# Reordering the loads and TensorE's work of batch 1 in a fused linear-attention and SwiGLU kernel

## The chip, the cores and the metric

The kernel runs on one core of a Trainium2 chip. The metric is the device time of one execution in microseconds (us), the median of several executions of the same program.

Engines: PE is TensorE's matmul stream and PEld its weight loads, DVE is VectorE, ACT ScalarE, POOL GpSimd, SP SyncE (which issues nearly all transfers here, 143 of 148 in the kernel before). A name with a q (SPq, PEldq) is an engine's sequencer. "L515" is a line of the kernel; the changed kernel's lines are higher by one or two.

## The reference, cut to what matters

```python
# q, k, v: (8 batches, 8 heads, 576 tokens, 64); weights 512 x 1536, 512 x 1536, 1536 x 512
kv  = einsum('bhsd,bhse->bhde', k, v)          # "states": one 64x64 matrix per head
out = einsum('bhsd,bhde->bhse', q, kv)
x   = out / sqrt(mean(out**2, -1) + 1e-6) * g_norm      # per head; then heads side by side: 4608 x 512
xn  = x / sqrt(mean(x**2, -1) + 1e-6) * moe_rms_g
y   = (silu(xn @ w_gate) * (xn @ w_val)) @ w_out        # 4608 x 512
```

All inputs and the output are fp32. The kernel computes in bf16 with fp32 accumulation.

## The kernel before

The work goes in nine units of 512 tokens (eight batches, then their tails together). A unit has 12 *up* steps (gate and value products, SiLU, product) and 48 *down* products. While PE does one unit's products, the attention of the next batch is slipped in between. The first unit has no unit ahead of it under which to hide the loads and preparations, so its order is written out by hand. The change touches that hand-written part: the first 57 of 324 us.

The parts that matter, shortened ("..." marks cuts):

```python
def load_wo(blk):                        # out weights come in three blocks of 4 chunks (1 MB each)
    st = stage()
    ap = st.rearrange("p (c d) -> p c d", d=d_model)
    nc.sync.dma_start(out=ap, in_=wo_view[:, 4 * blk : 4 * blk + 4, :])
    w_st["o", blk] = ap

# order of the loads
load_kv(1, "k", nc.sync); load_wo(0); load_kv(1, "v", nc.sync)
load_q(1); load_wo(1); load_wo(2); load_batch(2)

for j in range(4, NF):                   # up steps of the first unit
    ffn.up(j)
    ...                                  # casts of batch 1's keys and of out weights block 0 in between
for i in range(NS):
    cast_kv(1, "v", i, DVE if i % 2 else SC)
for i in range(4):
    cast_q(1, slice(2 * i, 2 * i + 2), SC if i == 2 else DVE)

def f_cols(j):                           # "columns": (q @ state) turned, one bank each; ACT squares them
    ps = att_pool.tile([128, MAIN], FP32, name="att_ps")       # a pool of two banks
    F.turned(j, ps)
    SC.activation(out=F.sq[:, j, :], in_=ps, func=ACT.Square)

down_part(0, 0, 4); down_part(1, 0, 4)   # down_part(c, lo, hi): chunks lo..hi of 128 tokens number c
att1.kv_products((0, 1, 2, 3)); att1.kv_copy()                 # states of batch 1
down_part(2, 0, 4)
turns.q_turn(0, SC); turns.q_turn(1, DVE)                      # turn of the queries on PE
down_part(3, 0, 4)
round_wo(1, 0, 2, DVE)                   # casts of out weights block 1 ...
...
f_cols(0); f_cols(1)
down_part(0, 4, 6); down_part(1, 4, 6)
f_cols(2); f_cols(3)
down_part(2, 4, 6); down_part(3, 4, 6)
F.sums()                                 # needs all four squares; then the normalisation of unit 1 begins
```

In the traces PE takes this work in the order written, and a group that is not ready holds what follows. In the kernel before, the turn began at 43.71 us and stood while its queries were cast, and the fourth down part, whose out weights the three parts ahead of it had used from 39.8 us on, began behind it, at 45.28.

## Time and profile before

Before: 325.77 us (median of 4 executions, 325.61 to 325.98); the profiled span is 323.6 us. PE is busy for 313.3 us of it (97%), at the full granted clock. The profile of the kernel before lacks the records of 34 of 1925 matmuls.

The windows view of the kernel before; columns are the stretch, its length, busy time and instruction count of each engine, granted PE clock, busy share of the DMA engines, GB/s:

```profile
core 0: us, PE busy (x) PEld busy (x) DVE busy (x) ACT busy (x) POOL busy (x), PEclk, DMA share, GB/s
0.00:26.00 26.00, 21.80 (x244) 14.35 (x248) 17.67 (x53) 14.21 (x27) 9.42 (x25) 1.00 1.00 324
26.00:39.59 13.59, 13.54 (x62) 6.17 (x63) 8.92 (x16) 7.25 (x13) 5.19 (x9) 1.00 1.05 384
39.59:57.00 17.41, 16.69 (x191) 9.30 (x192) 10.78 (x28) 10.44 (x18) 5.30 (x10) 1.00 1.09 332
57.00:300.00 243.00, 241.63 (x1285) 116.60 (x1310) 139.13 (x269) 139.56 (x250) 1.53 (x2) 1.00 0.55 141
```

After 57 us PE is all but full. Ahead of that the DMA engines are full (share 1.0 and more): weights and inputs stream in at 324 to 384 GB/s, and work that waits for a landing hangs on the order of that stream (the values of batch 1 landed at 40.2 us here, behind out weights block 0).

The chain of waits of the kernel before, 28 to 48 us (start, length, what):

```profile
28.11 15.09 DMA st<-in_q_dram
43.22 1.11 DVE qb L108 x3
...
45.48 0.69 DVE qt L108
46.17 0.97 DVE wo_sb L108
...
47.18 1.02 PE o_ps L515 x4
```

The queries of batch 1 land at 43.2 us. From there the chain goes through their casts, the copy of the turned queries and a cast of out weights before PE has work again at 47.18.

The timeline of the kernel before, a few groups of it (start, length, engine, line, operation; in brackets the idle time just before and what ended it):

```profile
41.41 1.32 PE L264 MATMUL att_ps<-vb,kb 64*64 64x64 bf16 x72
43.22 1.10 DVE L108 CAST qb<-st 128x512 bf16<-128x512 f32 x3 [1.56 <-DMA st<-in_q_dram]
43.71 1.74 PE L820 MATMUL att_ps<-identity,qb 128*128 128x128 bf16 x16
45.28 1.03 PE L515 MATMUL v_ps<-wo_sb,h_sb 128*128 128x512 bf16 x4
...
46.09 1.04 DVE L108 CAST wo_sb<-st 128x1024 bf16<-128x1024 f32 x1
46.23 0.60 PE L402 MATMUL att_ps<-qt,kv_all 128*128 128x512 bf16 x2
47.18 1.02 PE L515 MATMUL o_ps<-wo_sb,h_sb 128*128 128x512 bf16 x4 [0.35 <-DVE wo_sb L108]
...
49.62 0.55 PE L418 MATMUL att_ps<-sel,sqt 128*128 128x4 bf16 x16
...
57.01 1.03 PE L471 MATMUL g_ps<-xnt,wg_sb 128*128 128x512 bf16 x3
```

Read starts, not lengths, for PE: a 512-wide matmul is listed with 0.38 us, but the next one starts 0.216 us after it (groups of four follow each other every 0.86 to 0.87 us), so lengths overlap. The turn (L820, 16 small matmuls) holds PE from 43.71 to 45.28, 1.57 us, although such matmuls follow each other every 0.055 us elsewhere (16 of them from 17.62 to 18.51 us), because its queries are still being cast (DVE until 44.32). Two columns at 46.23 would take 0.43 us, but the next group starts at 47.18, when the out weights are cast. The last line, the first up product of the second unit at 57.01, is the milestone.

### The profile page before, as it was taken

The numbers are of one execution on the slowest core, as the hardware profiler recorded it, in microseconds if no ns is written. First come the engines' busy times: TensorE is split into PE (matmuls) and PEld (weight loads), VectorE is DVE, ScalarE is ACT, GpSimd is POOL, SyncE is SP. The second block draws the span as 40 slices with busy tenths as digits, with TensorE's granted clock in tenths as the row PEclk, the third lists the DMA queues.
The fourth block names the chain that finished last, engine by engine and source line by source line (L and its number), as shares of the span: only waits on it lengthen the run. The fifth ranks groups of instructions, "written<-read, shape, count | busy, mean of one in ns | idle before, by whom it ended". The sixth has DMA issues, their size and how long they took to land.

```text
span 323.6 us, 5091 instructions
## 1 busy us (share of the span) xinstructions
PE 313.3 (97%) x1891; PEld 156.5 (48%) x1925; DVE 180.9 (56%) x371; ACT 177.3 (55%) x316; POOL 21.5 (7%) x44
## 2 busy tenths in 40 slices
PE   7799999999999999999999999999999999999995
PEld 3485445554454445444544454444544444444443
DVE  4795756569527842685268616870588058803310
ACT  3476357756756576557665765666554355223321
POOL 1264324200000000000000000000000000000000
PEclk9999999999999999999999999999999999999999
DMA  7999999995279639952794279956101620150014
GB/s 261 347 350 386 379 373 289 250 280 144 54 195 286 151 65 181 303 137 49 189 313 133 46 153 199 312 138 158 69 2 27 151 83 0 21 172 6 0 34 98
DMA packets 75077, 54.87 MB, mean 170 GB/s; under 512 B 42152, under 2 KB 68012, under 8 KB 75052
## 3 DMA queue, kind: packets, MB, share of 16 engines
q1 hardware_dynamic: 74672, 53.88, 60.0%
q10 hardware_dynamic: 380, 0.66, 0.6%
q8 instruction: 15, 0.25, 0.3%
q14 instruction: 10, 0.08, 0.1%
HBM read 37.75 MB, written 9.44 MB: 146 GB/s over the span
## 4 chain that ended last, share of the span: by engine, by line
PE 81%; DMA 10%; DVE 3%; SPq 3%; issue 1%; POOL 0%; ACT 0%; DVEq 0%
PE o_ps L515 25%; PE g_ps L471 24%; PE v_ps L471 24%; DMA st<-in_q_dram 7%; DMA st<-in_moe_w_val_dram 3%; SPq L193 2%; PE att_ps L271 2%; PE att_ps L342 2%; DVE h_sb L477 1%; PE v_ps L515 1%; PE g_ps L515 1%; PE att_ps L337 0%; PE o_ps L552 0%; DVE ssq L360 0%; DVE qb L108 0%
## 5 line engine op out<-in xcount | busy, mean ns | idle before, releaser
L477 DVE TENSOR_TENSOR h_sb<-silu,v_ps 128x512 bf16<-128x512 bf16 x104 | 71.1, 684 | 110.4 <-PE v_ps L471 61.4
L471 PE MATMUL g_ps<-xnt,wg_sb 128*128 128x512 bf16 x403 | 105.1, 379 | 0.8 <-ACT wg_sb L201 0.2
L471 PE MATMUL v_ps<-xnt,wv_sb 128*128 128x512 bf16 x407 | 105.5, 379 | 0.4
L476 ACT ACTIVATE silu<-g_ps 128x512 bf16<-128x512 f32 x104 | 62.5, 601 | 64.1 <-PE g_ps L471 53.4
L515 PE MATMUL o_ps<-wo_sb,h_sb 128*128 128x512 bf16 x387 | 87.0, 379 | 0.8 <-DVE wo_sb L108 0.3
L471 PEld LDWEIGHTS <-wv_sb 128*128 128x128 bf16 x416 | 40.7, 98 | 49.1 <-DVE wv_sb L203 0.2
L515 PEld LDWEIGHTS <-h_sb 128*128 128x128 bf16 x420 | 40.7, 98 | 48.3 <-issue 0.6
L471 PEld LDWEIGHTS <-wg_sb 128*128 128x128 bf16 x416 | 38.7, 98 | 39.9 <-issue 0.3
L106 ACT COPY o_sb<-o_ps 128x512 f32<-128x512 f32 (+1 forms) x34 | 19.7, 579 | 38.1 <-PE o_ps L515 36.3
L360 DVE TENSOR_REDUCE ssq<-sq 128x16 f32<-128x1024 bf16 x28 | 34.1, 1220 | 1.0
L351 ACT ACTIVATE sq<-att_ps 128x512 bf16<-128x512 f32 x28 | 16.7, 597 | 13.7 <-PE att_ps L342 8.7
L106 ACT CAST vb<-st 128x512 bf16<-128x512 f32 (+2 forms) x34 | 19.5, 626 | 5.1 <-DMA st<-in_v_dram 5.1
L377 DVE TENSOR_TENSOR xna<-outa,s1y 128x512 bf16<-128x512 bf16 x28 | 17.5, 685 | 0.2
L353 ACT CAST outa<-att_ps 128x512 bf16<-128x512 f32 x28 | 16.2, 580 | 0.0
L106 ACT CAST qb<-st 128x1024 bf16<-128x1024 f32 (+1 forms) x15 | 14.2, 987 | 3.2 <-DMA st<-in_q_dram 3.2
L106 ACT CAST kb<-st 128x512 bf16<-128x512 f32 (+1 forms) x25 | 14.0, 619 | 0.0
L359 DVE TENSOR_TENSOR sq<-sq,gsq 128x512 bf16<-128x512 bf16 x28 | 11.7, 418 | 0.0
L342 PEld LDWEIGHTS <-qt 128*128 128x128 bf16 x96 | 7.4, 98 | 5.7
L342 PE MATMUL att_ps<-kv_all,qt 128*128 128x128 bf16 x96 | 9.3, 219 | 0.1
L271 PEld LDWEIGHTS <-kb 128*128 128x128 bf16 x120 | 7.7, 98 | 2.8
L612 PE MATMUL att_ps<-kv_all 128*128 128x512 bf16 (+1 forms) x19 | 6.9, 497 | 1.9 <-DVE sel L601 1.2
L271 PE MATMUL att_ps<-vb,kb 128*128 128x128 bf16 x120 | 8.7, 219 | 0.0
(134 smaller groups left out, 164.6 us busy)
## 6 DMA issues: line engine op xcount, KB each, us to landing
out_dram<-o_sb SPq DMA_DIRECT2D x16, 512.0 KB, 3.1
st<-in_q_dram SPq DMA_DIRECT2D x7, 1024.0 KB, 7.6
st<-in_k_dram SPq DMA_DIRECT2D x6, 1024.0 KB, 9.2
st<-in_v_dram SPq DMA_DIRECT2D x6, 1024.0 KB, 11.1
st<-in_moe_w_out_dram SPq DMA_DIRECT2D x3, 1024.0 KB, 13.5
st<-in_moe_w_gate_dram SPq DMA_DIRECT2D x4, 512.0 KB, 9.4
st<-in_moe_w_val_dram SPq DMA_DIRECT2D x4, 512.0 KB, 9.9
st<-in_k_dram SPq DMA_DIRECT2D x4, 288.0 KB, 5.2
```

What stands on the lines that cost most here:

```text
L106: engine.copy(out=dst, in_=src)
L271: PE.matmul(ps, lhsT=bufs[b]["k"][:, t, hs, :], rhs=bufs[b]["v"][:, t, hs, :], start=(first and t == 0), stop=(last and t == T),)
L342: PE.matmul(cols, lhsT=self.qt[:, j, 128 * c : 128 * c + 128], rhs=kv_all[:, self.n, j, :], start=(j == 0), stop=(j == NS - 1),)
L351: SC.activation(out=self.sq[c][:, 0], in_=ps, func=ACT.Square)
L353: SC.copy(out=self.outa[c], in_=ps)
L359: DVE.tensor_tensor(out=sq[:, 1], in0=sq[:, 0], in1=gsq8, op=OP.mult)
L360: DVE.reduce_sum(out=self.ssq[:, c], in_=sq, axis=AX.X)
L377: DVE.tensor_tensor(out=self.xna[c], in0=self.outa[c], in1=self.alpha[:, c, :].to_broadcast([128, H, D]), op=OP.mult)
L471: PE.matmul(ps, lhsT=wt[:, s, j * 128 : (j + 1) * 128], rhs=x[:, s, :], start=(s == 0), stop=(s == NS - 1),)
L476: SC.activation(out=silu, in_=g_ps, func=ACT.Silu)
L477: DVE.tensor_tensor(out=self.h[:, j, :], in0=silu, in1=v_ps, op=OP.mult)
L515: PE.matmul(self.o_ps[c], lhsT=self.h[:, j, c * 128 : (c + 1) * 128], rhs=wo_sb[:, j, :], start=(j == 0), stop=(j == NF - 1),)
```

## The change

Its intent: let everything that waits for a landing wait behind work that does not. The values of batch 1 are loaded ahead of the out weights, so that the states can run as soon as the up steps end; all 16 first down products stand between the states and the turn; out weights come in half loads, so that the first chunks of a block can be cast earlier; and the four columns get four banks, so that they need not wait for squares. At the very start, the gamma row is turned in another bank, and the rounding of one weight block is spread over three engines.

```diff
--- before.py
+++ after.py
@@ -207,7 +207,8 @@
     def load_wo(blk):
         st = stage()
         ap = st.rearrange("p (c d) -> p c d", d=d_model)
-        nc.sync.dma_start(out=ap, in_=wo_view[:, 4 * blk : 4 * blk + 4, :])
+        for i in (0, 2):
+            nc.sync.dma_start(out=ap[:, i : i + 2, :], in_=wo_view[:, 4 * blk + i : 4 * blk + i + 2, :])
         w_st["o", blk] = ap
 
     def round_wo(blk, i, n, engine):
@@ -695,7 +696,7 @@
     cast_kv(0, "v", 2, SC)
     put_q0(0, qps, 0, DVE)
     put_q0(0, qps, 1, SC)
-    gam_ps = att_pool.tile([128, 512], FP32, name="att_ps")
+    gam_ps = ops_pool.tile([128, 512], FP32, name="o_ps")
     PE.matmul(gam_ps[:, 0:5], lhsT=gam[0:5, :], rhs=ident32[0:5, 0:5], is_transpose=True, start=True, stop=True)
     DVE.tensor_copy(out=gcol, in_=gam_ps[:, NS : NS + 1])
     DVE.tensor_scalar(out=rowscale, in0=gam_ps[:, 0:NS], scalar1=gcol[:, 0:1], scalar2=None, op0=OP.mult)
@@ -760,10 +761,10 @@
     round_w(1, "g", 0, SC)
     round_w(1, "g", 3, SC)
     round_w(1, "g", 1, GP)
+    xs = [Z.scale(c, oZ[c]) for c in range(2)]
+    for s, engine in enumerate((GP, SC, DVE, DVE)):
+        round_w(1, "v", s, engine)
     SC.preload_act_table(ACT.Silu)
-    xs = [Z.scale(c, oZ[c]) for c in range(2)]
-    for s in range(NS):
-        round_w(1, "v", s, GP if s < 2 else DVE)
     clear_tail_rows(0, GP)
 
     def turnsZ():
@@ -778,9 +779,9 @@
             load_w(blk, name, nc.sync)
     alloc_kv(1, "k")
     load_kv(1, "k", nc.sync)
-    load_wo(0)
     alloc_kv(1, "v")
     load_kv(1, "v", nc.sync)
+    load_wo(0)
     load_q(1)
     load_wo(1)
     load_wo(2)
@@ -835,19 +836,22 @@
         if j == 6:
             for s in (0, 1):
                 round_w(4, "v", s, DVE)
-        if j >= 8:
-            cast_kv(1, "k", j - 8, DVE)
-        if j == 7:
-            for i in range(4):
-                round_wo(0, i, 1, GP)
-    for i in range(NS):
-        cast_kv(1, "v", i, DVE if i % 2 else SC)
-    for i in range(4):
-        cast_q(1, slice(2 * i, 2 * i + 2), SC if i == 2 else DVE)
+        if j == 9:
+            for i in range(3):
+                cast_kv(1, "k", i, DVE)
+        if j == 10:
+            cast_kv(1, "k", 3, DVE)
+            for i, engine in enumerate((SC, DVE, GP, DVE)):
+                cast_kv(1, "v", i, engine)
+    for i, engine in enumerate((SC, GP, DVE, SC)):
+        round_wo(0, i, 1, engine)
+    for i, engine in enumerate((DVE, SC, DVE, GP)):
+        cast_q(1, slice(2 * i, 2 * i + 2), engine)
     alloc_xnt(1)
 
     def f_cols(j):
-        ps = att_pool.tile([128, MAIN], FP32, name="att_ps")
+        p, nm = ((att_pool, "att_ps"), (att_pool, "att_ps"), (gps_pool, "g_ps"), (vps_pool, "v_ps"))[j]
+        ps = p.tile([128, MAIN], FP32, name=nm)
         F.turned(j, ps)
         SC.activation(out=F.sq[:, j, :], in_=ps, func=ACT.Square)
 
@@ -867,27 +871,21 @@
         round_wo(blk, 0, 2, DVE)
         round_wo(blk, 2, 2, SC)
 
-    down_part(0, 0, 4)
-    down_part(1, 0, 4)
     att1.kv_products((0, 1, 2, 3))
     att1.kv_copy()
-    down_part(2, 0, 4)
+    for c in range(4):
+        down_part(c, 0, 4)
     turns.q_turn(0, SC)
     turns.q_turn(1, DVE)
-    down_part(3, 0, 4)
-    round_wo(1, 0, 2, DVE)
-    for i in (2, 3):
-        round_wo(1, i, 1, GP)
-    for i in range(4):
-        round_wo(2, i, 1, GP)
+    for blk in (1, 2):
+        for i in range(4):
+            round_wo(blk, i, 1, GP)
     clear_tail_rows(1, GP)
     F = Cols(1, 0, 512, turns.qt, sqt_pool.tile([128, NS, MAIN], BF16, name="sqt"), "F")
-    f_cols(0)
-    f_cols(1)
     for c in range(2):
         down_part(c, 4, 6)
-    f_cols(2)
-    f_cols(3)
+    for j in range(NS):
+        f_cols(j)
     for c in range(2, 4):
         down_part(c, 4, 6)
     F.alloc_sums()
```

## The prediction

> **What bounds it.** The page gives PE busy 313.3 of 323.6 us at full granted clock. In the windows view PE is busy 241.6 of 243.0 us from 57 to 300 us; the change leaves that alone. Room is only ahead of 57 us: 26 to 39.6 us PE is busy 13.54 of 13.59 us; 39.6 to 57.0 us (down products and states, turns, columns of batch 1) 16.7 of 17.4, and the timeline shows more stalls inside its groups. That stretch hangs on the input DMA: its 16 engines are 90% busy in nearly all slices to 57 us, and the chain goes from the queries of batch 1 (issued 28.1, landed 43.2 us) over their casts (to 44.33), the turn (45.46), its copy (DVE, to 46.17) and the cast of out weights (DVE, to 47.13) to PE at 47.18.
>
> **Stalls before**, from the timeline: the turn holds PE 43.71 to 45.28, 1.57 us for 16 small matmuls that take 0.055 us each elsewhere (0.9 us): 0.7 lost, as PE reached it during the query casts. Two columns at 46.23, the next down products at 47.18: 0.5 lost to the out weight cast. With smaller gaps about 1.5 us.
>
> **What the change does.** Bytes, matmuls and casts stay. Transfers land 2.75 to 3 us apart per MB (37.3, 40.2, 43.2, 46.0, 48.7). Estimate after: values 37.5, out weights block 0 in halves 38.9 and 40.2, queries 43.2 unchanged (the DMA has a backlog), next halves 44.6 and 46.0. States run at 39.6 us (their casts end near 40.5: perhaps 0.1 lost), then all 16 down products (0.216 us each) to about 44.6. The query casts, now on three engines, end near 44.0, so the turn is stall-free, 44.6 to 45.5; before, turn and 16 products ended at 46.14. About 0.65 us gained. The products of chunks 4 and 5 then come ahead of the columns; POOL casts these chunks (0.63 us each) 44.6 to 45.9, so PE may lose 0.2 and ends 46.6. Four columns without a bank wait to 47.5; their squares on ACT (0.55 us each) run 47.0 to 49.2; the sums end near 49.35 against 50.0. The scaling chain on DVE and the rest follow about 0.65 us earlier.
>
> The start gains too (the third state no longer waits 0.7 us for the row scales, gamma being in another bank), but the landings at 43.2 to 46.0 absorb it. The SiLU table preload behind a 0.45 us cast costs nothing I see. [...] three more issues should cost nearly nothing.
>
> **Predicted**: 325.1 us (0.65 less), range 324.4 to 325.7; faster by over 2%: 0.01; within 2%: 0.98; slower: 0.01.
>
> **To check.** Right if: the turn takes PE about 0.9 us; PE's wait for the out weight cast is gone; queries land at 43.2 +-0.5; the second unit's first up product (57.01 before) starts near 56.3; what follows stays as long.
>
> **What would make it wrong.** Half loads slow the DMA stream or change its order, so that queries or out weights come later. POOL, alone with out weights of blocks 1 and 2, holds the down products longer. Squares end after 49.2 and the sums wait. Or the start's gain does move later landings: up to 1.3 us. Values of batch 2 land at 59.9, their state is needed at 62.2: little slack if all moves earlier.

The clause that three more issues should cost nearly nothing is the author's estimate, from the landings 2.75 to 3 us apart per MB.

## The result, and the profile after

After: 325.04 us (median of 4 executions, 324.71 to 325.17) against 325.77 us before, 0.73 us less. The ratio is 0.9976, 95% interval 0.9958 to 0.9993: clear of noise. (Ratios here are the mean time of one kernel's fast runs over that of the other's of the same rounds, so not quite the ratio of the medians.) A second measurement (c0 below) gives 325.03 against 325.64 us. The profiled span went from 323.6 to 323.1 us.

The windows view of the changed kernel, the same columns:

```profile
26.00:39.59 13.59, 13.59 (x64) 6.06 (x62) 9.49 (x17) 7.87 (x15) 4.23 (x7) 1.00 1.05 385
39.59:57.00 17.41, 17.32 (x199) 9.96 (x198) 10.99 (x29) 11.07 (x20) 6.77 (x12) 1.00 1.09 333
```

PE is now busy 17.32 of 17.41 us in the stretch where the view before gives 16.69; but that one lacks records of matmuls (191 against 199 here), so the starts below carry the reading. The DMA stream is as it was (333 GB/s).

The timeline of the changed kernel, the groups that answer to those above (the last three ACT groups are the squares):

```profile
39.74 1.52 PE L265 MATMUL att_ps<-vb,kb 64*64 64x64 bf16 x72
41.19 1.90 PE L516 MATMUL o_ps<-wo_sb,h_sb 128*128 128x512 bf16 x8
...
43.20 1.18 DVE L108 CAST qb<-st 128x512 bf16<-128x512 f32 x2 [1.72 <-DMA st<-in_q_dram]
43.23 0.87 POOL L108 CAST qb<-st 128x512 bf16<-128x512 f32 x1 [3.74 <-DMA st<-in_q_dram]
44.66 1.06 PE L821 MATMUL att_ps<-identity,qb 128*128 128x128 bf16 x16
45.55 1.06 PE L516 MATMUL o_ps<-wo_sb,h_sb 128*128 128x512 bf16 x4
46.50 0.60 PE L403 MATMUL att_ps<-qt,kv_all 128*128 128x512 bf16 x2
46.92 1.09 ACT L856 ACTIVATE sqt<-att_ps 128x512 bf16<-128x512 f32 x2 [0.61 <-PE att_ps L403]
47.90 0.60 ACT L856 ACTIVATE sqt<-g_ps 128x512 bf16<-128x512 f32 x1
48.37 0.62 ACT L856 ACTIVATE sqt<-v_ps 128x512 bf16<-128x512 f32 x1
48.52 0.78 PE L419 MATMUL att_ps<-sel,sqt 128*128 128x4 bf16 x16
...
56.13 1.03 PE L472 MATMUL g_ps<-xnt,wg_sb 128*128 128x512 bf16 x4
```

Side by side, the query casts took 0.43 and 0.84 us on DVE and 0.87 on POOL. In the kernel before, with POOL idle, they took 0.42 us each on DVE, and POOL takes 0.61 for casts of the same shape at 47.26 us, with DVE idle. No run isolates it, so that is all that can be said.

The queries land when they did (43.20). The turn now starts at 44.66, behind all down products and behind the casts, and the next group starts 0.89 us later, not 1.57. No wait of PE for out weights is left. Two short ones are left. The states take 1.45 us from their start to the next group, 1.26 before, because one of the value casts is late (e8 moves it to another engine and has 1.26 again). And the sums (48.52) wait, as their last part needs the last square (48.99). The second unit begins at 56.13 us, 0.88 us earlier. But the span shrank by only 0.5 us, so something after 57 us, where nothing was changed, gave 0.4 us back. The position of PE's down products in the third unit and after it shows where: 112.85 us before and 112.02 after, but 145.94 before and 145.53 after. The gap of 0.83 falls to 0.41 us within one unit. The changed kernel's waits name the place:

```profile
PE g_ps L472 <- DMA xnt<-xna: 0.2, 1, 0.2
```

Until 122.79 us PE waited for a transposing transfer (the normalised tokens of the next unit are turned by DMA, four transfers per unit). By starts the wait is 0.4 us: the 48 down products from 112.02 us on, 0.216 us each, end at 122.39. From the view by tile of these transfers in that unit, first the kernel before (issues: shortest, median, longest, first and last start; then time from issue to landing):

```profile
L384 SPq DMA_TRANSPOSE xnt<-xna x4: 1209/1222/1249, 115.5 to 119.5; - x4
DMA to landing us min/median/max: 2.5/2.5/2.5
```

and the changed kernel:

```profile
L385 SPq DMA_TRANSPOSE xnt<-xna x4: 1204/1220/1237, 114.7 to 118.6; - x4
DMA to landing us min/median/max: 2.4/2.4/4.1
```

One of four landed 1.6 us late. Of the 28 such transfers in each of the two profiles, four in each of seven units, it is the only one above 2.5 us. Whether this is chance or belongs to the change was the open question that the experiments took up beside the main ones.

### The profile page after: what moved, and what is told of

Its sections match the earlier page's. It is cut to its first block, busy times and chain, and to the rows that moved or that the text cites. A ratio compares the mean times of both kernels' runs of the same rounds, so it can differ in the third digit from the quotient of the medians.

```text
span 323.1 us, 5133 instructions
## 1 busy us (share of the span) xinstructions
PE 315.9 (98%) x1925; PEld 156.8 (49%) x1925; DVE 180.9 (56%) x370; ACT 178.1 (55%) x318; POOL 21.2 (7%) x44
## 4 chain that ended last, share of the span: by engine, by line
PE 85%; DMA 7%; DVE 4%; SPq 1%; ACT 1%; issue 1%; DVEq 0%
PE g_ps L472 27%; PE v_ps L472 27%; PE o_ps L516 23%; DMA st<-in_moe_w_gate_dram 3%; PE att_ps L272 2%; DMA st<-in_q_dram 2%; PE att_ps L343 2%; DMA xnt<-xna 1%; DVE h_sb L478 1%; DVE xna L378 1%; PE g_ps L516 1%; PE v_ps L516 1%; DMA out_dram<-o_sb 1%; ACT sqt L856 1%; SPq L385 1%
## 5 line engine op out<-in xcount | busy, mean ns | idle before, releaser
L472 PE MATMUL g_ps<-xnt,wg_sb 128*128 128x512 bf16 x416 | 106.8, 380 | 0.2 <-DMA xnt<-xna 0.2
L472 PE MATMUL v_ps<-xnt,wv_sb 128*128 128x512 bf16 x416 | 106.8, 379 | 0.0
```

The costliest lines, as they stand in the source:

```text
L472: PE.matmul(ps, lhsT=wt[:, s, j * 128 : (j + 1) * 128], rhs=x[:, s, :], start=(s == 0), stop=(s == NS - 1),)
```

## The experiments

Twelve kernels ran, each in five or six executions beside the kernel before; all gave correct results. The experiments start from the changed kernel. "Against changed" compares medians with c0's 325.03 us. "Stretch" runs from the end of the last up product of the first unit to the first up product of the second (start of the last value group plus its four products, 0.86 us); "third unit" is the distance of the first down products of the third and fourth unit. Both are from the one profiled execution, and neither contains the start, which lies up to 0.8 us apart between the profiles (last value group at 38.41 us in e1, at 39.17 in e5).

| kernel | median us | kernel before | ratio | against changed | stretch | third unit | longest of the four landings there |
|---|---|---|---|---|---|---|---|
| before | | | | | 17.42 | 33.09 | 2.5 |
| changed, first run | 325.04 | 325.77 | 0.9976 | | 16.49 | 33.51 | 4.1 |
| c0 changed again | 325.03 | 325.64 | 0.9982 | 0 | 16.52 | 33.38 | 4.0 |
| e1 start undone | 325.16 | 325.64 | 0.9985 | +0.13 | 16.69 | 33.50 | 4.1 |
| e2 values behind | 325.98 | 325.64 | 1.0011 | +0.95 | 17.60 | 33.34 | 4.0 |
| e3 whole loads | 325.94 | 325.64 | 1.0009 | +0.91 | 17.84 | 33.09 | 2.5 |
| e4 two banks | 325.89 | 325.61 | 1.0001 | +0.86 | 17.28 | 33.46 | 4.1 |
| e5 turn early | 325.48 | 325.61 | 0.9998 | +0.45 | 17.23 | 33.30 | 3.9 |
| e6 columns first | 325.85 | 325.61 | 1.0004 | +0.82 | 17.15 | 33.39 | 4.0 |
| e8 gaps closed | 324.48 | 325.61 | 0.9963 | -0.55 | 16.20 | 33.52 | 4.0 |
| e9 eight more | 324.70 | 325.61 | 0.9973 | -0.33 | 16.50 | 33.09 | 2.5 |
| e10 gaps and eight | 324.51 | 325.61 | 0.9969 | -0.52 | 16.22 | 33.09 | 2.5 |
| e11 one halved | 324.76 | 325.61 | 0.9976 | -0.27 | 16.64 | 33.09 | 2.5 |
| e12 gaps, one halved | 324.64 | 325.90 | 0.9963 | -0.39 | 16.51 | 33.09 | 2.5 |

The rows lie in four calls, each on a chip of its own, and the 95% intervals of the ratios are about +-0.0013 (0.4 us) wide. Differences of 0.3 us between rows are therefore only indicated by the medians; where I call them shown, the positions in the profile carry it.

### c0: the changed kernel again

No edit.

> Control: the changed kernel once more, beside the kernel before on the same chip. Expected 325.0 us +-0.2, 0.7 us under the kernel before, and again the first up product of the second unit near 56.1 us. In the first profile of this kernel one of 28 transposing transfers landed after 4.1 us instead of 2.4 and cost PE 0.25 to 0.4 us at 122.8 us. If that belongs to the changed kernel (its new order of transfers), it is there again in the same place; if it is chance, it is gone or elsewhere, and the span is then near 322.7.

It came again: 325.03 us, milestone 56.16, and the same one transposing transfer of the third unit late, after 4.0 us. So it is not chance. It costs 0.29 us here and 0.42 in the first profile (third unit 33.38 and 33.51 against 33.09 us).

### e1: the start's two edits undone

```diff
-    gam_ps = ops_pool.tile([128, 512], FP32, name="o_ps")
+    gam_ps = att_pool.tile([128, 512], FP32, name="att_ps")
...
-    xs = [Z.scale(c, oZ[c]) for c in range(2)]
-    for s, engine in enumerate((GP, SC, DVE, DVE)):
-        round_w(1, "v", s, engine)
     SC.preload_act_table(ACT.Silu)
+    xs = [Z.scale(c, oZ[c]) for c in range(2)]
+    for s in range(NS):
+        round_w(1, "v", s, GP if s < 2 else DVE)
```

> Undoes both edits of the start: gamma turned in a bank of the attention pool again, and the values weights of block 1 rounded and the table loaded in the old order. Theory: the start's 0.46 us (third state earlier) is given back at 21 us, where PE waits for the rounding of weights that landed at 20.1 us, and only 0.1 to 0.2 us of it is left at 26 us: total +0.1 to +0.2 us. Rival: the start carries over half of the gain: +0.4 us or more.

Measured +0.13 us, in the forecast range but within the spread (324.73 to 325.61), so the start's worth is about nothing. The traces of before and after say why. The timeline of the kernel before at two places of the start:

```profile
17.62 1.05 PE L488 MATMUL g_ps<-xnt,wg_sb 128*128 128x128 bf16 x16
22.05 1.03 PE L488 MATMUL o_ps<-xnt,wg_sb 128*128 128x256 bf16 x8
```

and of the changed kernel:

```profile
17.17 1.05 PE L489 MATMUL g_ps<-xnt,wg_sb 128*128 128x128 bf16 x16
20.42 0.97 DVE L203 TENSOR_SCALAR wv_sb<-st,rowscale 128x256 bf16<-128x256 f32 x2
21.45 0.72 PE L489 MATMUL v_ps<-xnt,wv_sb 128*128 128x256 bf16 x5 [0.17 <-DVE wv_sb L203]
22.10 1.03 PE L489 MATMUL o_ps<-xnt,wg_sb 128*128 128x256 bf16 x8
```

PE is 0.45 us earlier at 17 us, and 0.05 us later at 22 us: it waits for value weights that landed at 20.1 us and that DVE rounds until 21.39. The profile of c0 confirms it: there PE is at the first place at 16.79 us, and at the last at 22.11 all the same.

### e2: values behind the out weights

```diff
+    load_wo(0)
     alloc_kv(1, "v")
     load_kv(1, "v", nc.sync)
-    load_wo(0)
```

> Undoes the load order alone: out weights block 0 (in halves) ahead of the values of batch 1. Theory: values land near 40.2 instead of 37.5 us, their casts end near 41.5, and PE, which wants the states at 39.6, stands 1 to 1.8 us: total +0.9 to +1.5 us against the changed kernel, so slower than the kernel before. Rival (the load order matters little, as casts could follow): within 0.3 us of the changed kernel.

Measured +0.95 us; the stretch is 1.1 us longer. PE's waits from 38 to 50 us in this run hold one line:

```profile
PE att_ps L265 <- ACT vb L106: 1.2, 1, 1.2
```

The states wait 1.2 us for the cast of the values. With the states first, the load order is needed; the theory stands.

### e3: whole loads of out weights

```diff
-        for i in (0, 2):
-            nc.sync.dma_start(out=ap[:, i : i + 2, :], in_=wo_view[:, 4 * blk + i : 4 * blk + i + 2, :])
+        nc.sync.dma_start(out=ap, in_=wo_view[:, 4 * blk : 4 * blk + 4, :])
```

> Undoes the half loads alone: out weights in three transfers of 1 MB. Theory: block 1 is seen at 46.0 instead of 44.6 us for its first half, POOL casts chunks 4 and 5 until 47.2, and the down products of these chunks, which now stand ahead of the columns, hold PE about 1 us more: total +0.8 to +1.1 us. Rival: the halves are for show, within 0.2 us.

Measured +0.91 us, as expected, but as a sum of two parts. The stretch is 1.35 us longer; the only waits that the view lists for PE from 40 to 50 us are

```profile
PE o_ps L515 <- POOL wo_sb L108: 1.2, 2, 1.1
```

for the casts of chunks 4 and 5. Against that the late transposing transfer is gone (2.5 us, third unit 33.09), which gives back about 0.4 us. That was the first hint that the half loads bring it.

### e4: columns over two banks

```diff
-        p, nm = ((att_pool, "att_ps"), (att_pool, "att_ps"), (gps_pool, "g_ps"), (vps_pool, "v_ps"))[j]
+        p, nm = (att_pool, "att_ps")
```

> Undoes the four banks alone: the four columns go through the two banks of the attention pool again. Theory: columns 3 and 4 wait for the squares of 1 and 2 (about 0.6 to 0.8 us of PE), but the sums wait for the squares on ACT in both kernels, so little of it reaches the end: +0.0 to +0.3 us. Rival: the whole wait counts, +0.6 us or more.

Measured +0.86 us, stretch +0.8: the rival is right, and my expectation was wrong. The timeline of this run:

```profile
46.62 0.60 PE L403 MATMUL att_ps<-qt,kv_all 128*128 128x512 bf16 x2
47.04 2.15 ACT L856 ACTIVATE sqt<-att_ps 128x512 bf16<-128x512 f32 x4 [0.61 <-PE att_ps L403]
47.69 0.86 PE L403 MATMUL att_ps<-qt,kv_all 128*128 128x512 bf16 x2 [0.47 <-ACT sqt L856]
```

The squares end at 49.19, hardly later than in the changed kernel (48.99). I had concluded that the sums, which wait for them, would hide PE's wait. But the sums waited only some 0.25 us in the changed kernel; here PE reaches them 1.02 us later (49.35 instead of 48.33), and all but those 0.25 us counts.

### e5: the turn ahead of the fourth down part

```diff
-    for c in range(4):
+    for c in range(3):
         down_part(c, 0, 4)
     turns.q_turn(0, SC)
     turns.q_turn(1, DVE)
+    down_part(3, 0, 4)
```

> Puts the turn of the queries back ahead of the fourth down part. Theory: PE reaches the turn at 43.8 instead of 44.66 us, while the query casts run (43.2 to 44.4): 0.4 to 0.6 us lost in the turn, seen as a turn of 1.3 to 1.5 us; part of it can come back as the out weight casts are then further along: +0.2 to +0.6 us. Rival: the turn's place does not matter, within 0.1 us.

Measured +0.45 us, stretch +0.7. In this run's timeline the turn stalls on the query casts as in the kernel before, 1.54 us from its start to the next group at 45.91:

```profile
44.37 0.31 PE L821 MATMUL att_ps<-identity,qb 128*128 128x128 bf16 x2
45.01 1.06 PE L821 MATMUL att_ps<-identity,qb 128*128 128x128 bf16 x14 [0.33 <-DVE qb L108]
```

This shows the first cause of the gain: four down products ahead of the turn instead of behind it. (The stretch of this profile also holds 0.2 us at the states, 1.65 us instead of 1.45, which the edit does not touch; so the 0.45 us of the medians is the better measure.)

### e6: all columns ahead of the second down parts

```diff
-    for c in range(2):
-        down_part(c, 4, 6)
     for j in range(NS):
         f_cols(j)
-    for c in range(2, 4):
+    for c in range(4):
         down_part(c, 4, 6)
```

> Puts all four columns directly behind the turn, and all down products of chunks 4 and 5 after them. Theory: PE waits for the copy of the turned queries (0.6 to 0.8 us, to about 46.3), but then has the down products to cover the squares, so the wait of the sums (0.25 us) is gone: net +0.2 to +0.5 us. Rival: the order of columns and down products is neutral, within 0.1 us.

Measured +0.82 us, stretch +0.65, above the forecast. From the timeline of this run:

```profile
46.70 0.60 PE L403 MATMUL att_ps<-qt,kv_all 128*128 128x512 bf16 x2 [0.79 <-DVE qt L108]
```

The direction was right (PE waits for the copy of the turned queries), the size was not: the wait cost 0.95 us from the end of the turn (45.75, sixteen starts at 0.055 us after 44.86) to 46.70. So the two down parts ahead of the columns are the cover for that copy, and their weights must be there by then, which is what the half loads buy (e3).

### e8: closing the gaps that are left

```diff
-    for s, engine in enumerate((GP, SC, DVE, DVE)):          # rounding of value weights, block 1
+    for s, engine in enumerate((GP, SC, GP, DVE)):
...
-            for i, engine in enumerate((SC, DVE, GP, DVE)):  # casts of batch 1's values
+            for i, engine in enumerate((SC, SC, GP, DVE)):
...
-        SC.activation(out=F.sq[:, j, :], in_=ps, func=ACT.Square)
+        if j == 1:
+            raw = silu_pool.tile([128, MAIN], BF16, name="silu")
+            DVE.tensor_copy(out=raw, in_=ps)
+            DVE.tensor_tensor(out=F.sq[:, j, :], in0=raw, in1=raw, op=OP.mult)
+        else:
+            SC.activation(out=F.sq[:, j, :], in_=ps, func=ACT.Square)
...
+    round_wo(1, 1, 1, DVE)                                   # chunk 5; POOL leaves it out below
     turns.q_turn(0, SC)
```

> Tries to beat both kernels by closing the gaps that the changed kernel's trace still shows: third quarter of the block 1 value weights rounded on POOL instead of DVE, second value cast on ACT instead of DVE, chunk 5 of the out weights cast on DVE instead of POOL, and the square of column 2 on DVE (copy, then multiply). Theory: 0.25 us at the sums, 0.1 to 0.3 us at the states, up to 0.3 us at the start, limited by the landings of queries (43.2) and of the first half of block 1 (44.6): -0.2 to -0.6 us, about 324.6 us. Rival: landings already bind everywhere, within 0.1 us.

Measured -0.55 us: 324.48 us, faster than the kernel before, also by the interval of its ratio (0.9951 to 0.9975); and all five executions (324.25 to 324.68) lie under all five of c0 (324.82 to 325.47), though on another chip. In its profile the stretch is 0.3 us shorter: the states take 1.26 us from their start (39.48) to the down products (40.74) instead of 1.45, and the sums 0.41 us instead of 0.64. Against that the turn takes 1.03 us instead of 0.89, as PE now reaches it while the last query cast runs. The rest would be the start, about 0.26 us earlier at the end of the up products (last group at 38.52 us instead of 38.78); but e2, which has the start of the changed kernel, is also there at 38.52, so that this part is not shown to come from the edits. Its transposing transfer is late again (4.0 us).

### e9 to e11: why one transposing transfer lands late

All kernels with six half loads had the late transfer, the two without did not. What could three more transfers at 25 to 39 us do to one at 118 us? In the program and in the trace the transfers use eight completion semaphores in turn (called 0 to 7 here). Three more transfers shift which of the eight each later transfer gets. In the built program, PE waits for the four transposing transfers of the fourth unit by semaphore number, highest first: a wait instruction of its sequencer asks for the two highest numbers, the first weight load for the next, the first matmul for the lowest. In the kernel before, the four transfers have the numbers 3, 4, 5 and 6, so the highest is that of the last. In the changed kernel they have 6, 7, 0 and 1, so the highest is that of the second, and the last is asked for only by the weight load.

The start of the wait instruction shows this. The kernel before (lengths in ns, shortest, median and longest of two; start of the first and of the second, which is the one in question):

```profile
L471 PEldq EVENT_SEMAPHORE  x2: 51/51/51, 90.0 to 121.9; - x2
```

and the changed kernel:

```profile
L472 PEldq EVENT_SEMAPHORE  x2: 51/1966/3880, 85.4 to 118.5; - x2
```

The 3880 ns are easily taken for the second of the two. They belong to the first, at 85.4 us, a unit earlier; the same view from 112 us on has the second alone:

```profile
L472 PEldq EVENT_SEMAPHORE  x1: 51/51/51, 118.5 to 118.5; - x1
```

Before, the instruction starts only at 121.9, when the last transfer has landed (issued 119.5, 2.5 us). After, it starts at 118.5, as the second transfer, which it now asks for first, has landed (issued near 116.0, 2.4 us), and it is over in 51 ns, as the first landed near 117.1. The DMA view has 15 instruction packets of 16 KB in every profile, 0.9 to 1.8 us each. One of them started at 124.0 us in the kernel before and at 124.7 in e3, but at 119.3 to 120.7 us in each kernel with six half loads: in the midst of the last transposing transfer. So I supposed that the order of the waits sets the time of this packet, and that the packet holds up a part of the transfer that it runs beside. That was an estimate from these starts and landings alone; no trace shows how the one would bring the other. If it is right, restoring the old order of semaphores must cure the late landing without removing a single half load. Adding five more transfers makes eight, a full round:

```diff
-        for i in (0, 2):
-            nc.sync.dma_start(out=ap[:, i : i + 2, :], in_=wo_view[:, 4 * blk + i : 4 * blk + i + 2, :])
+        for i, n in (((0, 1), (1, 1), (2, 2)) if blk == 0 else [(i, 1) for i in range(4)]):
+            nc.sync.dma_start(out=ap[:, i : i + n, :], in_=wo_view[:, 4 * blk + i : 4 * blk + i + n, :])
```

> The changed kernel, but its out weights come in 3, 4 and 4 transfers instead of 2, 2 and 2: eight more transfers than the kernel before, so that transfers from there on use the same of the eight completion semaphores as in the kernel before. Theory: in all seven kernels with half loads so far a 16 KB instruction packet ran at 119.1 to 120.5 us, during the last transposing transfer of the third unit, which landed after 4.0 us and held PE 0.25 to 0.4 us; in the two without it ran at 124 us, after it. The reason would be the order in which PE waits on those four semaphores: with the last transfer's first (kernel before), the sequencer stands there until it has landed, and the fetch comes later. Here that order is restored: instruction packet near 123 us, last transposing transfer lands after 2.4 to 2.5 us, no wait of PE there, total -0.3 to -0.4 us against the changed kernel (near 324.65). Rival: the number of weight transfers as such or the earlier time of the unit brings the collision: still 4 us, no gain.

Measured -0.33 us (324.70), no late transfer (2.5 us), the third unit back at 33.09, and the stretch unchanged (16.50). The instruction packet ran at 123.1 us. The DMA view from 117 to 123 us in 40 slices of 0.15 us (busy share in tenths, then GB/s), first the changed kernel:

```profile
DMA  0299961000599940060799999000000000988999
GB/s 0 65 215 220 213 145 16 0 0 0 111 229 217 215 99 4 0 109 5 145 196 208 198 64 0 0 0 0 7 10 9 10 9 14 410 218 300 382 437 328
```

and e9:

```profile
DMA  1899920002999710004999500489999799939995
GB/s 22 179 215 222 195 42 0 0 0 53 208 220 217 155 21 0 0 0 102 220 213 218 113 7 0 191 355 382 410 382 410 300 437 382 249 80 198 247 231 100
```

The humps are the transposing transfers. In the changed kernel the 16 KB packet (the 109 GB/s slice, counted when it starts) precedes the last hump, and over half a microsecond after that hump 7 to 14 GB/s trickle in, from 121.2 to about 122.1 us. The packet ran from 119.66 to 121.23 us, so the trickle begins when it ends. Of the 512 packets of 256 B (128 KB) of that transfer, 478 start from 119.8 to 120.6 us, none from then to 121.2, and the last 34, 8.7 KB, one after the other to 122.1; in the kernel before all 512 start from 120.7 to 121.4 us. The 34 are about a sixteenth of the 512, and take about 8% of the time of the 16 DMA engines from 121.25 to 122.1 us. So I take them for the part of one engine, but no record names the engine: that is my estimate. The packet records of all eight profiles with a late landing show the same: some 8.7 KB of the transfer move only after the 16 KB packet is over. In e9 the hump ends at once, and the store follows.

e11 halves only block 1, one transfer more than before. The expectation below takes it that PE's first wait then falls on the third of the four. In the built program that is so a unit earlier; in the unit in question the numbers are 4, 5, 6 and 7, and the first wait falls on the last, as in the kernel before:

```diff
-        for i in (0, 2):
-            nc.sync.dma_start(out=ap[:, i : i + 2, :], in_=wo_view[:, 4 * blk + i : 4 * blk + i + 2, :])
+        for i, n in (((0, 2), (2, 2)) if blk == 1 else ((0, 4),)):
+            nc.sync.dma_start(out=ap[:, i : i + n, :], in_=wo_view[:, 4 * blk + i : 4 * blk + i + n, :])
```

> The changed kernel with half loads for block 1 of the out weights alone, blocks 0 and 2 whole. Theory for the early stretch: only block 1 needs halves, as its first chunks are wanted right after the turn; first up product of the second unit at 56.1 to 56.4 us as in the changed kernel. For the transposing transfer: PE's first wait is now on the third of the four, which lands about 1.3 us ahead of the last, so the instruction packet would come near 121 us, too late to do harm: landing 2.4 to 2.8 us, total -0.2 to -0.4 us against the changed kernel. Rival: all three blocks need halves, then block 0's casts hold the down products at 41 to 42 us and the total is +0.2 us or more.

Measured -0.27 us, no late transfer, third unit 33.09, stretch 16.64. So the halves of blocks 0 and 2 are worth at most 0.15 us in the stretch. The forecast of the landing came true, but by a misread order: the wait instruction starts at 121.5 us, when the last transfer has landed, and the packet ran at 123.75 us, not at 121. That fits the link rather than weakens it. In the eight profiles with a late landing the wait instruction starts at 118.1 to 119.6 us and the packet 1.0 to 1.9 us after it; in the six without, at 120.7 to 122.5 us and the packet 2.1 to 2.2 us after it. Which instruction sets off the packet I did not find out.

e10 joins e8's edits and e9's loads:

> The edits that closed the gaps (324.48 us) and the 3, 4 and 4 transfers together. If both stand on their own: no late transposing transfer, first up product of the second unit near 55.6 us, total near 324.1 us. If the collision comes again, near 324.5.

Its profile has both gains (stretch 16.22, third unit 33.09) and the shortest span of all, 322.3 us. It also excludes that the time at which the unit runs is what brings the collision: e8 starts the third unit's down products at 111.50 us and has the late transfer, e10 at 111.51 and has none. But its median is 324.51 us (324.17 to 325.04), not 324.1, and no better than e8's. The positions say that the gains add; the five totals do not show it, and why two of the five executions took over 324.8 us I don't know.

### e12: e8's edits with e11's loads

> The edits that closed the gaps together with half loads for block 1 alone: one transfer more than the kernel before. If the two gains stand on their own: first up product of the second unit at 55.6 to 55.9 us, instruction packet near 123 us, no late transposing transfer in the third unit, total 324.1 to 324.4 us. With block 0 whole, its casts start at 40.1 us instead of 38.8 and could hold the down products, which the edits let start at 40.7 us: then up to 0.3 us of it is lost.

324.64 us, ratio 0.9963 as e8. The packet came at 123.1 and no transfer was late, but the milestone was at 55.91 us, the late end of the forecast, and the stretch 16.51 us. The ratios of e8, e10 and e12 to the kernel before, 0.9963, 0.9969 and 0.9963, cannot be told apart. All three beat the kernel before by 1.1 to 1.3 us by the medians, and their medians are 0.4 to 0.55 us under the changed kernel's.

## Why the prediction was right, and where its parts were not

- **The total**: 325.1 us predicted (324.4 to 325.7), 325.04 measured. It is partly luck: the touched stretch gained more than predicted (0.93 us, 17.42 to 16.49, instead of 0.65), and 0.42 us was lost where I had said "what follows stays as long".
- **The turn** "about 0.9 us, stall-free, 44.6 to 45.5": 44.66 to 45.55. Right, and e5 shows the cause by undoing it.
- **The queries at 43.2**, "the DMA has a backlog": 43.20. Right. That three more issues cost nearly nothing on the DMA stream is right for the first 57 us (332 and 333 GB/s from 39.59 us on).
- **The wait for the out weight cast** gone: right; e3 shows that it comes back with 1.2 us when the halves go.
- **Down products of chunks 4 and 5** "ends 46.6": 46.50. **Columns** to 47.5: 47.37. **Squares** to 49.2: 48.99. **Sums** near 49.35: 49.16. Each a little early, which carries through to a milestone of 56.13 instead of "near 56.3".
- **The start** "gains too, but the landings at 43.2 to 46.0 absorb it": it gains nothing that lasts, but it is absorbed much earlier, at 21 us, by value weights that landed at 20.1 us and that DVE rounds until 21.39. The end of the up products is at 38.73 plus 0.86 us before and 38.78 plus 0.86 after.
- **"What follows stays as long"** failed. I had asked whether the half loads could delay the stream or change the order of landings; I had not thought of a transfer 80 us later. e3, e9 and e11 show that the number of transfers decides it, though not by growing: 3, 4 and 11 transfers of out weights have no late landing, 6 have one. A 16 KB instruction packet ran during the transfer in each of the eight profiles with a late landing (from 119.3 to 120.7 us on) and after it in each of the six without (122.9 us or later), and some 8.7 KB of the transfer moved only behind it. With the late landing the third unit took 33.30 to 33.52 us instead of 33.09. That the packet holds up one engine's part is my estimate. That the order of PE's semaphore waits is the link is supported by e9's forecast coming true and by the starts of the wait instruction in all 14 profiles, but not shown directly; which instruction sets off the packet is open.
- After the fact, the worth of the parts, from undoing each alone: load order 0.95 us, half loads 0.9 (1.35 in the stretch), four banks 0.86, turn behind the down parts 0.45, start about 0.1. Their sum is far more than the whole change brings. They are links of one order, each needed for the others: undoing one leaves the other moves in place without their cover.

## What to carry to other kernels

In a stream that is bound by one engine that takes its work in the order written (here PE, 97% busy), put work that needs nothing new in front of each step that waits for a landing, and move all of it together: the load order, the size of the loads, the banks and the place of the work each cost about as much alone as the whole move gains (0.45 to 0.95 us, the whole 0.73). Before you call a wait hidden behind another, subtract: only as much of it is hidden as the other wait measures (0.25 us in e4, not 1). After a change, compare the positions of the untouched rest too: here three more transfers at 25 to 39 us shifted waits on semaphores at 118 us, and one transfer 1.6 us late took back almost half of this gain (0.42 of 0.93 us). And where a view gives shortest, median and longest of two, narrow the window before you say which of the two was the long one.
